# Tiles chosen in registers, x tiles that carry their own history, and result rows behind the running sum

## The chip, the core and the metric

The kernel runs on one core of a Trainium2 chip. A core has five engines with instruction streams of their own: TensorE (PE) multiplies matrices into PSUM, VectorE (DVE) and ScalarE (ACT) do elementwise work, GpSimd (POOL) does elementwise work on SBUF and issues the indirect DMAs, and SyncE (SP) issues nearly all other DMAs. Sixteen DMA engines are shared by all queues. PSUM has 8 banks of 512 float words in each of 128 partitions. The metric is the device time of one execution in microseconds (us); lower is better.

## The reference

The kernel computes a weighted sum over a window of 7 rows, and then a mixture of 8 experts in which each row goes to one.

```python
# x: (8, 3584, 192), weight_gen: (8, 3584, 8 heads, 7 taps)
w = softmax(weight_gen, axis=-1)
x_pad = concatenate([zeros(6 rows), x], axis=1)
out[b, s, h, :] = sum_k w[b, s, h, k] * x_pad[b, s + k, h, :]   # 24 columns a head

x = out.reshape(28672, 192)
logits = x @ w_gate                                   # 8 experts
e = argmax(logits); p = softmax(logits)[e]
eom = sigmoid(x @ w_output_gate)[e]
y = p * eom * (relu(x @ w1[e]) @ w2[e])               # 192 -> 1024 -> 192
```

All arrays are float32. The kernel multiplies in float16 with each operand split into a high and a low half, three products in place of one.

## The kernel before, in words

**Units.** A batch is laid out with partition p holding rows 28p to 28p + 27. A unit u is 7 of these 28 rows on every partition, so 896 rows; there are 4 units to a batch and 32 in all. For each unit DVE and ACT take the softmax of its weights (`softmax_steps`), POOL multiplies x by the weights of taps 0 to 4 (0 to 3 in units 0 to 6) and DVE by those of the others (`product`, `tap_steps`). Tap k of row j needs row j - 6 + k, which for small j lies in the tile of the unit before it or, in a batch's first unit, in a tile `halo` loaded from the partition above. So each product is made of two instructions, one on the old rows and one on the new.

**The sum.** In units 0 to 6 PE adds the seven products up through an identity matrix. From unit 7 on (`PE_U = 7`, `acc_steps`) DVE adds them in place into one running sum in PSUM words 2560 to 3903, which lie in banks 5, 6 and 7: one product is written there and six are added. `sum_steps` then reads the sum four times: ACT squares it and copies it to float16, DVE takes the low halves in two instructions. The float16 row `rt` is turned by DMA (`gt`), PE makes the logits, DVE picks the expert, and two small matmuls (`rk`) give each row its place in its expert's list. POOL scatters the rows to these places in DRAM (`srtd`), seven indirect DMAs a unit.

**Tiles.** As soon as lists hold enough rows, tiles of 512 rows of one expert are taken from them (256 and 384 early, 512 to 128 at the end; 76 tiles in all, their sizes fixed by `plan_rounds`). Which expert each tile takes is worked out at run time. `round_table` does it on DVE, on one partition, in some ten small instructions for a unit: it compares the eight counts with what was taken already, scans them and leaves the expert and the first row of each tile in a small table `ti`. SP loads these two numbers into registers (`value_load`, seen as TENSOR_LOAD) when it issues the tile's loads in `tile_load`: the rows' tokens and scales (`meta`), the rows turned (`xT`), and the expert's weights (`wa`, `wb`), each load waiting for every scatter that has been issued by then.

**The two multiplications.** `gemm_steps` sets PE's order. At each beat PE runs two units of the first multiplication (`gemm1_unit`: for a 512-row tile five matmuls of 512 columns into one bank) and one group of the second (`gemm2_group`: 24 matmuls of 192 columns for 128 result rows). ACT and DVE turn a finished bank into `hh` (relu, high half) and `hl` (low half). ACT scales a finished group into `ys`, and POOL scatters it to the output. Both multiplications take their banks from one list, `bank_free`: the banks at words 0, 512, 1024 and 1536, and four more once no unit is left. From the time that bank 1536 joins, the logits and the rank matmuls also take a bank of this list.

**What sets the order.** The kernel is written out by a planner (`Order`, `Queue`, `Paced`) while it is built. Each step is a generator with a due time; the planner keeps a clock for each engine, adds an estimated cost to it at every instruction (`vector_cost`, `scalar_cost`, `gpsimd_cost`, `sync_cost`) and always runs the step that could start first. The engines then run their streams in this fixed order, and the tile framework adds the semaphore waits between them. Every instruction that the planner records carries the line of its helper (L151 on the engines, L125 on SP).

Of the kernel before, what the change touches and what calls it, by code (L numbers as in the profile page):

```python
# [20 lines left out]
RMAX = 24  # L21
SHIFT = 15
NE = 8
# [32 lines left out]
def constants():  # L56

    ident = np.eye(P, dtype=np.float32)
    upper = np.triu(np.ones((P, P), np.float32), 1)
    r = np.arange(RMAX, dtype=np.float32)  # L60
    rr = np.tile(r[:, None], (1, 9))
    need = [T * r for T in (128, 256, 384, 512)]
    e8 = np.arange(8, dtype=np.float32) - 8.0
    flat = np.concatenate([rr.ravel(), *need, e8]).astype(np.float32)
    return np.concatenate([ident, upper, np.tile(flat[None], (P, 1))], axis=1)
# [41 lines left out]
class Queue:  # L107
# [6 lines left out]
    @property  # L114
    def t(self):
        if self.host is not None:
            return self.host.t
        return max(self.moved, self.issued + self.lead)

# [58 lines left out]
def vector_cost(name, args, kwargs):  # L178
    n = largest(args, kwargs)
    return 0.06 + n / 156.0 if name == "reciprocal" else 0.07 + n / 960.0  # L180


def scalar_cost(name, args, kwargs):
    return (0.19 if "accum_out" in kwargs else 0.1) + largest(args, kwargs) / 1200.0


def gpsimd_cost(name, args, kwargs):
    if name == "indirect_dma_start":
        return 1.2 if LOCK else 1.04
    if name == "memset":  # L190
        return 1.0
    return (0.14 if LOCK else 0.06) + largest(args, kwargs) * (0.0022 if kwargs.get("op") == ALU.add else 0.00174)
# [13 lines left out]
def sync_cost(name, args, kwargs):  # L206
# [6 lines left out]
    return n / 360e3 * (1.25 if name == "dma_start_transpose" else 1.0)  # L213
# [4 lines left out]
def kernel(ctx: ExitStack, tc: tile.TileContext, x, wg, wgate, wogate, w1, w2, cst, out):  # L218
# [47 lines left out]

    def take_place(slots):
# [20 lines left out]
    f_mx = few[:, 80:136]  # L288
    f_lim = few[0:1, 189:190]

    f_next = few[0:1, 136:152].rearrange("p (e r) -> p e r", r=2)
    f_z = few[0:1, 152:170].rearrange("p (e r) -> p e r", r=2)
    f_done = f_next[:, :, 0]
    f_ex = ps[:, 2536:2538].bitcast(I32)
    f_rr = ps[0:1, 2512 : 2512 + RMAX]

    rest_free = [(0.0, 3904), (0.0, 1344)]
    mx_free, few_free, sq_free = [0.0], [0.0], [0.0]
# [26 lines left out]
    def x_load(u):  # L325
        b, q = u // UB, u % UB
        xb = x[b].rearrange("(p j) d -> p j d", j=J)
        if q == 0:
            for lo, hi in ((1, 113), (113, 128)):
                SP.dma_start(out=halo[lo:hi], in_=xb[lo - 1 : hi - 1, J - HALO : J, :])  # L330
# [3 lines left out]
    halo = xp.tile([P, HALO, D], F32, name="halo")  # L334
    nc.gpsimd.memset(halo[0:1], 0.0)
# [7 lines left out]
    cf = cp.tile([P, cst.shape[1]], F32, name="cf")  # L343
    nc.scalar.dma_start(out=cf, in_=cst)
# [14 lines left out]
    o = 256  # L359
    rr = cf[0:1, o : o + RMAX * 9].rearrange("p (a b) -> p a b", b=9)  # L360
    o += RMAX * 9
    need = {}
    for k in (128, 256, 384, 512):
        need[k] = cf[0:1, o : o + RMAX]
        o += RMAX
    nc.vector.tensor_copy(f_e8, cf[:, o : o + 8])
# [3 lines left out]
    for e in range(NE):  # L370
        nc.vector.memset(base[:, e : e + 1], float(e * CAP - 1))
        nc.vector.memset(f_done[:, e : e + 1], float(e * CAP))


    cs = cp.tile([1, 1 + 8 * RMAX], F32, name="cs")
    nc.vector.memset(cs[:, 0:1], 0.0)
    nc.vector.memset(f_z[:, 8, :], float(DUMMY))
    nc.vector.tensor_copy(f_rr, rr[:, :, 0])
# [9 lines left out]
    state = {"base": base, "writers": [], "t": 0, "weights": 0, "rounds": 0}  # L388

# [142 lines left out]
    def product(eng, out, u, k):  # L532

        n, w4, wk = HALO - k, wloads[u], k
        if eng is V:
            w4, wk = U[u]["tw"], k - U[u]["tw_k"]
        old = halo[:, k:HALO, :] if u % UB == 0 else loads[u - 1][:, k + 1 : JS, :]
        for lo, hi, xs in ((0, n, old), (n, JS, loads[u][:, 0 : JS - n, :])):
            if hi > lo:
                eng.tensor_tensor(  # L540
                    out=out[:, lo * H : hi * H, :], in0=xs.rearrange("p j (h g) -> p (j h) g", g=GD),
                    in1=w4[:, lo * H : hi * H, wk : wk + 1].broadcast_to([P, (hi - lo) * H, GD]), op=ALU.mult)

    def softmax_steps(u):

        w4 = wloads[u]
        mxb = f_mx.unsqueeze(2).broadcast_to([P, NV, K])
        yield from take(mx_free, V)
# [21 lines left out]
        mx_free.append(od.cur.t)  # L570
# [80 lines left out]
    def used(u, tag):  # L651
# [5 lines left out]
        if "va" in d and "ga" in d:  # L657
            t = max(d["va"], d["ga"])
            x_free.extend([t] * ((u % UB > 0) + (u % UB == UB - 1)))
            w_free.append(max(d["va"], d["ga"]))  # L660
# [19 lines left out]
    def sum_steps(u):  # L680
# [84 lines left out]
        od.add(place_steps(u), (RANK_C, u, 0), V)  # L765

# [67 lines left out]

    def place_steps(u):
# [11 lines left out]
        d["rk_home"].append((od.cur.t, d["rk_at"]))  # L847
        d["ranked"] = True
        if u in plan:
            od.add(round_steps(u), (RANK_R, u), V)  # L850
        else:
            state["rounds"] += 1
# [20 lines left out]
        d["sent"] = True  # L873
        d["sent_t"] = od.cur.t + 2.5
        rt_free.append((d["sent_t"], d["ri"]))


    def round_table(r, T, R, tail, bs):

        nm = f"{r}"  # L880
        rT = need[T][:, 0:R].unsqueeze(1).broadcast_to([1, 8, R])
        if R > 2:
            n = R
            nx = sp.tile([1, 8, RMAX], F32, tag="nx", bufs=1, name=f"nx{nm}")[:, :, 0:R]
            z = sp.tile([1, 9, RMAX], F32, tag="z", bufs=1, name=f"z{nm}")[:, :, 0:R]
            V.memset(z[:, 8, :], float(DUMMY))
            V.tensor_tensor(out=nx, in0=f_done.unsqueeze(2).broadcast_to([1, 8, R]), in1=rT, op=ALU.add)
            state["step"] = None
            yield V
        else:  # L890
            if state.get("step") != T:
                state["step"] = T if R == 2 else None
                if R == 2:
                    V.tensor_scalar(f_next[:, :, 1], f_done, float(T), None, op0=ALU.add)
                    yield V
            n = 2 if state["step"] == T else 1
            nx, z = f_next[:, :, 0:n], f_z[:, :, 0:n]

        gg = sp.tile([1, 8 * RMAX], F32, tag="gg", bufs=1, name=f"gg{nm}")[:, 0 : 8 * R]
        V.scalar_tensor_tensor(out=gg.rearrange("p (e r) -> p e r", r=R), in0=bs[0:1, :].unsqueeze(2).broadcast_to([1, 8, R]), scalar=0.0 if tail else 1.0 - T, in1=nx[:, :, 0:R], op0=ALU.add, op1=ALU.is_ge)  # L900
        yield V

        if state.get("limit") != R:
            V.memset(f_lim, float(R))
            state["limit"] = R
        V.tensor_tensor_scan(out=cs[:, 1 : 1 + 8 * R], data0=gg, data1=f_lim.broadcast_to([1, 8 * R]), initial=0.0, op0=ALU.add, op1=ALU.min)
        yield V
        cx = cs[:, 0 : 1 + 8 * R : R]

        V.scalar_tensor_tensor(out=z[:, 0:8, :], in0=cx[:, 0:8].unsqueeze(2).broadcast_to([1, 8, n]), scalar=-float(T), in1=nx, op0=ALU.mult, op1=ALU.add)  # L910
        ge = sp.tile([1, RMAX, 9], F32, tag="ge", bufs=1, name=f"ge{nm}")[:, 0:R, :]
        V.tensor_tensor(out=ge, in0=cx.unsqueeze(1).broadcast_to([1, R, 9]), in1=f_rr[:, 0:R].unsqueeze(2).broadcast_to([1, R, 9]), op=ALU.is_le)
        yield V
        n = 1 if R > 2 else n
        V.scalar_tensor_tensor(out=f_next[:, :, 0:n], in0=cx[:, 1:9].unsqueeze(2).broadcast_to([1, 8, n]), scalar=float(T), in1=z[:, 0:8, 0:n], op0=ALU.mult, op1=ALU.add)
        V.tensor_tensor(out=ge, in0=ge, in1=z[:, :, 0:R].rearrange("p e r -> p r e"), op=ALU.mult)
        yield V
        if R > 8:
            ti = sp.tile([1, 2, RMAX], I32, tag="til", bufs=1, name=f"ti{nm}")
        else:  # L920
            ti = sp.tile([1, 2, 8], I32, tag="ti", bufs=NU // 2 + 6, name=f"ti{nm}")
        with nc.allow_low_precision(reason="whole numbers"):
            V.tensor_reduce(out=ti[:, 1, 0:R], in_=ge, axis=AX, op=ALU.max)
        yield V
        V.tensor_scalar(ti[:, 0, 0:R], ti[:, 1, 0:R], SHIFT, None, op0=ALU.arith_shift_right)
        yield V
        return ti
# [3 lines left out]
    def round_steps(u):  # L931

        found, bs = [], U[u]["base"]
        yield V, lambda: state["rounds"] == u
        for k, (T, R) in enumerate(plan[u]):
            tail = u == NU - 1 and k == len(plan[u]) - 1
            pads = None
            if tail:
                pads = sp.tile([1, NE], I32, tag="bi", name="bi")
                bf = sp.tile([1, NE], F32, tag="bf", name="bf")  # L940
                V.tensor_scalar(bf, bs[0:1, :], 1.0, None, op0=ALU.add)
# [322 lines left out]
XN = 4  # L1264
# [38 lines left out]
```

## Time and profile before

| what | value |
|---|---|
| three runs | 1226.5, 1228.21, 1228.29 us, median 1228.21 |
| the profiled execution | 1230.08 us, its span 1228.0 us |
| mean granted TensorE clock | 0.974 |
| busy in the span | PE 1132.9, DVE 956.4, POOL 879.8, ACT 594.5 us |
| PE idle, waiting for DVE's `hl` | 38.1 us, 40 times |
| SP waiting for scatters to `srtd` | 170.7 us, 44 times |
| first and last result read (`ys`) | 190.2 and 1220.5 us |
| last unit's sum read for the last time | 967.6 us |

The page gives busy time by engine, the chain of work that ended last, the waits and the costliest groups of instructions. A group is read as: engine, operation, what it writes and reads by the program's names, shape, count, then busy us and mean ns of one, then the idle time just before it and what ended it. `ps` is all of PSUM, so a row `ps<-ps,gap` on DVE is an addition to the running sum. Three stretches of the span follow each other: up to about 178 us the first seven units and the preparation of the weights, up to 969 us units and tiles side by side, and after it tiles alone.

### The profile page before, as it was taken

To read this page: it belongs to the slowest core of one execution; us is meant where nothing else is said; L and a number is where in the kernel's file an instruction comes from. 1 tells how busy PE (TensorE), PEld (TensorE's weight loads), DVE (VectorE), ACT (ScalarE), POOL (GpSimd) and SP (SyncE) were. 2 spreads that over 40 slices of the span, in tenths; PEclk is the share of its full clock that TensorE was granted. 3 is DMA by queue.
4 is the path that set the end of the run, shared out by engine and by line. 5 is a ranking of instruction groups with operands and counts; after the bars stand their busy time and mean duration, and the time that the engine had idled before them with its cause. 6 is when DMAs were issued, how large, how long until landed. Compare 5 with 4: busy or idle time off the path is not lost.

```text
span 1228.0 us, 27900 instructions
## 1 busy us (share of the span) xinstructions
PE 1132.9 (92%) x9710; PEld 821.3 (67%) x9710; DVE 956.4 (78%) x2027; ACT 594.5 (48%) x1263; POOL 879.8 (72%) x778
## 2 busy tenths in 40 slices
PE   5988779899999999899999999899998999999997
PEld 2444448677666666676766666676666777988987
DVE  6898759899999898998998999899998663333331
ACT  3875345455555445454544454445544544344342
POOL 5668786668888788888888988888887663322222
PEclk9998989899999999999999999999999999999999
DMA  9998378999989869698769759997777679889992
GB/s 281 284 283 288 131 237 196 262 277 250 247 232 240 206 182 248 150 262 211 213 191 229 208 154 244 231 234 188 207 203 185 178 219 278 235 255 330 272 310 80
DMA packets 278047, 279.73 MB, mean 228 GB/s; under 512 B 211479, under 2 KB 236808, under 8 KB 277905
## 3 DMA queue, kind: packets, MB, share of 16 engines
q1 hardware_dynamic: 256016, 233.35, 69.1%
q0 software_dynamic: 21744, 44.30, 13.3%
q8 instruction: 76, 1.25, 0.4%
q14 instruction: 67, 0.54, 0.1%
q10 hardware_dynamic: 144, 0.29, 0.1%
HBM read 177.07 MB, written 60.87 MB: 194 GB/s over the span
## 4 chain that ended last, share of the span: by engine, by line
PE 40%; DVE 26%; POOL 12%; issue 8%; DMA 7%; SPq 3%; ACT 3%; POOLq 0%; DVEq 0%; ACTq 0%
PE ps L151 40%; DVE ps L151 11%; POOL gap L151 6%; DVE hl L151 5%; POOL srtd L151 3%; SPq L125 3%; DMA srtd<-rt,posi 2%; POOL out_dram L151 2%; DMA wa<-wd 2%; DVE rt L151 2%; DMA gt<-rt 1%; DVE vap L151 1%; ACT rt L151 1%; DVE ti L151 1%; DVE vt L151 1%
## 5 line engine op out<-in xcount | busy, mean ns | idle before, releaser
L151 PE MATMUL ps<-xT,wa 128*128 128x512 f16 (+3 forms) x2440 | 493.0, 350 | 42.7 <-DVE hl L151 33.3
L151 PE MATMUL ps<-wb,hh 128*128 128x192 f16 x3664 | 478.9, 248 | 4.8 <-DVE hl L151 4.8
L151 PE MATMUL ps<-wb,hl 128*128 128x192 f16 x1832 | 454.1, 248 | 0.1
L151 DVE SCALAR_TENSOR_TENSOR hl<-ps,hh 128x512 f16<-128x512 f32 (+1 forms) x472 | 307.5, 665 | 156.3 <-ACT hh L151 155.9
L151 POOL TENSOR_TENSOR gap<-x,w 128x960 f32<-128x960 f32 (+5 forms) x268 | 360.0, 1368 | 37.1 <-DVE lz L151 9.2
L151 ACT ACTIVATE hh<-ps 128x512 f16<-128x512 f32 (+1 forms) x472 | 272.1, 582 | 226.1 <-PE ps L151 223.5
L151 PEld LDWEIGHTS <-wa 128*128 128x128 f16 x2440 | 226.5, 99 | 226.7 <-issue 48.8
L151 PEld LDWEIGHTS <-hh 128*128 128x128 f16 x3664 | 337.0, 99 | 50.5 <-issue 9.4
L151 POOL DMA_INDIRECT out_dram<-ys,meta x216 | 214.5, 993 | 193.6 <-ACT ys L151 146.3
L151 POOL DMA_INDIRECT srtd<-rt,posi x224 | 229.0, 1022 | 87.0 <-issue 56.4
L151 DVE TENSOR_TENSOR ps<-ps,gap 128x1344 f32<-128x1344 f32 x125 | 194.2, 1554 | 21.8 <-POOL gap L151 21.8
L151 ACT ACTIVATE ys<-ps,sc 128x192 f32<-128x192 f32 x229 | 96.3, 421 | 221.0 <-PE ps L151 160.5
L151 PEld LDWEIGHTS <-hl 128*128 128x128 f16 x1832 | 180.9, 99 | 0.6 <-DVE hl L151 0.3
L151 PE MATMUL ps<-gap,cf 128*128 128x512 f32 x168 | 72.9, 569 | 3.2 <-DVE vap L151 3.2
L151 PE MATMUL ps<-vap,cf 128*128 128x512 f32 (+1 forms) x126 | 58.2, 603 | 13.5 <-DVE vap L151 12.9
L151 POOL TENSOR_TENSOR gap<-halo,w 128x1152 f32<-128x1152 f32 (+4 forms) x38 | 60.4, 1589 | 13.2 <-issue 5.7
L151 DVE SCALAR_TENSOR_TENSOR rt<-ps,sx,rt 128x448 f16<-128x448 f32 x64 | 57.9, 908 | 10.4 <-ACT rt L151 5.8
L151 PE MATMUL ps<-xT,late 128*128 128x128 f16 (+2 forms) x600 | 56.6, 251 | 0.0
L151 ACT ACTIVATE rt<-ps 128x1344 bf16<-128x1344 f32 x32 | 41.3, 1291 | 28.2 <-issue 18.3
L151 PEld LDWEIGHTS ps<-gap,cf 128*128 128x128 f32 x168 | 31.4, 199 | 34.8 <-issue 25.6
L151 PEld LDWEIGHTS ps<-vap,cf 128*128 128x128 f32 x126 | 24.9, 208 | 38.7 <-issue 22.9
L151 ACT ACTIVATE rt<-ps,sx 128x1344 f16<-128x1344 f32 x32 | 44.2, 1380 | 9.6 <-DVE isx L151 7.6
(123 smaller groups left out, 841.8 us busy)
## 6 DMA issues: line engine op xcount, KB each, us to landing
wb<-wd SPq DMA_DIRECT2D x76, 768.5 KB
wa<-wd SPq DMA_DIRECT2D x61, 768.0 KB
x<-in_x_dram SPq DMA_DIRECT2D x32, 672.0 KB
late<-wd SPq DMA_DIRECT2D x15, 768.0 KB
wa<-wd SPq DMA_DIRECT2D x61, 128.0 KB
w<-in_wg_dram SPq DMA_DIRECT2D x32, 196.0 KB
wd<-wpb SPq DMA_DIRECT2D x8, 768.5 KB
st<-in_w_dram SPq DMA_DIRECT2D x8, 768.0 KB
```

The source lines that it names most:

```text
L125: r = f(*args, **kwargs)
L151: r = f(*args, **kwargs)
```

## The change

**Tiles in registers.** `round_table` is gone. ACT writes the eight counts of a unit as integers (`count_steps`, one more ACT instruction a unit, `cnt`), SP loads them into eight registers (`counted`), and `pick` chooses for each tile the expert with the most rows left, in register instructions of SP's own stream. A tile's loads wait for the scatters up to its own unit, not for all that were issued.

**x tiles.** A tile of x holds 13 rows a partition, the unit's 7 and the 6 before them, so a product is one instruction, and a tile is free after its own unit (`XN` 4 to 3). A load is 1248 KB where it was 672 KB; a batch's first unit loads the six rows above from a tile of zeros on partition 0.

**Result rows.** PSUM words 3904 to 4095, 192 words behind the running sum, held weights of the early units. Once these are done they become a place for one result group (`out_free`), and `take_out` gives it out ahead of the banks. The rank results keep their words in bank 4.

**The planner's costs** are changed to other numbers, and with them the order on all engines.

```diff
-        loads[u] = xp.tile([P, JS, D], F32, tag="x", bufs=XN, name=f"x{u}")
-        SP.dma_start(out=loads[u], in_=xb[:, q * JS : (q + 1) * JS, :])
+        t = loads[u] = xp.tile([P, HALO + JS, D], F32, tag="x", bufs=XN, name=f"x{u}")
...
+            SP.dma_start(out=t, in_=x[b].rearrange("(p j) d -> p j d", j=J)[:, q * JS - HALO : q * JS + JS, :])
...
-        old = halo[:, k:HALO, :] if u % UB == 0 else loads[u - 1][:, k + 1 : JS, :]
-        for lo, hi, xs in ((0, n, old), (n, JS, loads[u][:, 0 : JS - n, :])):
-            if hi > lo:
-                eng.tensor_tensor(
...
+        eng.tensor_tensor(
+            out=out, in0=loads[u][:, k : k + JS, :].rearrange("p j (h g) -> p (j h) g", g=GD),
+            in1=w4[:, :, wk : wk + 1].broadcast_to([P, NV, GD]), op=ALU.mult)
...
+    def counted(cnt):
+
+        R.reg_load(came, cnt[0:1, 0:NE])
+        for e in range(NE):
+            R.reg_alu(key[e], key[e], came[e], ALU.add)
+        SP.spend(0.6)
+
+    def pick(T):
+
+        R.reg_mov(best, (T - 1 << HAVE) + (DUMMY >> ROW))
+        for e in range(NE):
+            R.reg_alu(best, best, key[e], ALU.max)
+        for e in range(NE):
+            R.reg_alu(came[e], key[e], best, ALU.is_ge)
+            R.reg_alu(came[e], came[e], (T >> ROW) - (T << HAVE), ALU.mult)
+            R.reg_alu(key[e], key[e], came[e], ALU.add)
+        R.reg_alu(best, best, low, ALU.bitwise_and)
+        SP.spend(1.1)
+        return R.snap(best, min_val=0, max_val=DUMMY >> ROW)
...
+    def count_steps(u):
+
+        cnt = U[u]["cnt"] = sp.tile([1, NE], I32, tag="cnt", bufs=CNT, name=f"cnt{u}")
+        S.activation(cnt, U[u]["rk"][0:1, 8:16], AF.Copy, scale=float(1 << HAVE))
...
+        d["writers"] = list(state["writers"])
...
-            d = tile_load(state["t"], T, ti, i, list(state["writers"]), ka, kb)
+            d = tile_load(state["t"], T, at, U[u]["writers"], ka, kb)
...
+    def take_out():
+
+        yield T_, lambda: out_free or bank_free
+        home = out_free or bank_free
+        t, at = home.pop(0)
+        od.cur.t = max(od.cur.t, t)
+        yield T_
+        return at, home
...
-                _, at = yield from take(bank_free, T_)
+                at, home = yield from take_out()
...
+        yield T_, lambda: any(f[1] == 3904 for f in rest_free)
+        rest_free.remove(next(f for f in rest_free if f[1] == 3904))
+        out_free.append((od.cur.t, 3904))
         yield T_, lambda: "all" in state
+        yield from take(out_free, T_)
         bank_free.extend((od.cur.t, at) for at in (2560, 3072, 3584, 2048))
...
-        for _ in range(2):
-            yield from take(rk_free, T_)
...
-    return 0.06 + n / 156.0 if name == "reciprocal" else 0.07 + n / 960.0
+    return 0.15 + n / 156.0 if name == "reciprocal" else 0.15 + n / 960.0
```

Three places in the order of the two programs show what moved. In the rows a name carries its tile's number, the first number of `gap16_3` being the unit and the second the tap, that of `hl20_6` the tile and the unit of its first multiplication; in brackets are the engines and queues whose semaphores an instruction waits for.

DVE before, at the running sum of unit 16:

```order
L151 TENSOR_TENSOR ps_82<-ps_82,gap16_0_6453 128x1344 [waits DVE_49,Pool_49]
L151 SCALAR_TENSOR_TENSOR hl20_0_6595<-ps_82,hh20_0_6594 128x512 [waits Activation_49]
L151 TENSOR_TENSOR ps_82<-ps_82,gap16_1_6487 128x1344 [waits DVE_49,Pool_49]
L151 SCALAR_TENSOR_TENSOR hl20_1_6605<-ps_82,hh20_1_6604 128x512 [waits Activation_49]
L151 TENSOR_TENSOR ps_82<-ps_82,gap16_2_6591 128x1344 [waits DVE_49,Pool_49]
L151 SCALAR_TENSOR_TENSOR hl20_2_6651<-ps_82,hh20_2_6650 128x512 [waits Activation_49]
L151 TENSOR_TENSOR ps_82<-ps_82,gap16_3_6647 128x1344 [waits DVE_49,Pool_49]
L151 SCALAR_TENSOR_TENSOR hl20_3_6662<-ps_82,hh20_3_6661 128x512 [waits Activation_49]
```

DVE in the change, at the same additions:

```order
L155 TENSOR_TENSOR ps_82<-ps_82,gap16_0_6897 128x1344 [waits Activation_49,Pool_49]
L155 SCALAR_TENSOR_TENSOR hl20_6_7223<-ps_82,hh20_6_7222 128x512 [waits Activation_49]
L155 TENSOR_TENSOR ps_82<-ps_82,gap16_1_6941 128x1344 [waits DVE_49,PE_49,Pool_49]
L155 SCALAR_TENSOR_TENSOR hl20_7_7242<-ps_82,hh20_7_7241 128x512 [waits Activation_49]
L155 TENSOR_TENSOR ps_82<-ps_82,gap16_2_7001 128x1344 [waits Activation_49,Pool_49]
L155 SCALAR_TENSOR_TENSOR hl21_0_7280<-ps_82,hh21_0_7279 128x512 [waits Activation_49]
L155 SCALAR_TENSOR_TENSOR hl21_1_7293<-ps_82,hh21_1_7292 128x512 [waits Activation_49]
L155 TENSOR_TENSOR ps_82<-ps_82,gap16_3_7085 128x1344 [waits DVE_49,PE_49,Pool_49]
L155 TENSOR_TENSOR ps_82<-w17_6265,ps_82 128x112
L155 TENSOR_TENSOR ps_82<-ps_82,gap16_4_7238 128x1344 [waits Activation_49,Pool_49]
```

Before, an addition waits for DVE itself and for POOL, which makes `gap`. In the change each waits for PE or for ACT as well: the instructions waited for are the result groups of tiles 19 and 20 and their reads, which lie in the words from 3904 on, in bank 7 with the end of the sum.

ACT in the change, from the third result read of tile 19 on:

```order
L155 ACTIVATE ys19_6965<-ps_82,sc19_6966 128x192 [waits DVE_49,PE_49]
L155 ACTIVATE hh20_6_7222<-ps_82 128x512 [waits PE_49]
L155 ACTIVATE hh20_7_7241<-ps_82 128x512 [waits PE_49]
L155 ACTIVATE ys19_6965<-ps_82,sc19_6966 128x192 [waits DVE_49]
L155 ACTIVATE hh21_0_7279<-ps_82 128x512 [waits PE_49]
L155 ACTIVATE hh21_1_7292<-ps_82 128x512 [waits PE_49]
L155 ACTIVATE sc20_7304<-meta20_6405,wb20_6411 128x4 [waits DMAHW3_49]
L155 ACTIVATE ys20_7303<-ps_82,sc20_7304 128x192 [waits DMASW4_49,DMASW6_49,DMASW2_49,DMASW7_49,DVE_49,Activation_49]
```

The reads `ys` now wait for DVE too, for the addition that stands ahead of them in bank 7; before, no read waits for an addition. On PE a result group's first matmul waits likewise for the addition or the read that comes before it. Counted through the order of the change, from the first group in these words to the last read of unit 31's sum: 170 groups, 170 result reads, 173 writes of the sum (24 products and 149 additions) and 100 reads of it (50 on ACT, 50 on DVE), in one fixed sequence, which begins behind unit 7's first product and first addition. PE has 19039 rows in either program, and POOL 153 products where it had 306 pieces of them. Before, no group lies in this bank until the last unit is done; all lie in banks 0 to 3.

SP before, from the last write of prepared weights to the first tile's first load:

```order
L125 DMA wd_79<-wpb7_1081 128x1537
L125 DMA w8_1216<-in_wg_dram 128x392
L125 DMA halo_83<-in_x_dram 112x1152
L125 DMA halo_83<-in_x_dram 15x1152
L125 DMA x8_1221<-in_x_dram 128x1344
L125 TENSOR_LOAD ti2_0_1128
L125 ISA x2
L125 TENSOR_LOAD ti2_0_1128
L125 ISA x3
L125 DMA meta0_1361<-srtd_78 128x2x2
```

SP in the change, from the same write on:

```order
L129 DMA wd_79<-wpb7_1483 128x1537
L988 ISA
L129 DMA meta0_1531<-srtd_78 128x2x2
L129 ISA
L129 DMA_TRANSPOSE xT0_1533<-srtd_78 128x3x256
L129 ISA
L129 DMA wa2_136<-wd_79 128x1536
```

The first tile's loads moved ahead of unit 8's, which now stand ahead of that write; the two TENSOR_LOADs of a tile are gone.

More of the change, by code (lines that the diff above doesn't have):

```diff
@@ L20 @@
 WW = 3585
-RMAX = 24
+TURNS = 240
 SHIFT = 15
+ROW = 7
+HAVE = 11
 NE = 8
@@ L118, in t, with spend @@
         return max(self.moved, self.issued + self.lead)
+    def spend(self, us):
+        self.issued = max(self.issued, self.order.now) + us
     def __getattr__(self, name):
@@ L929 @@
     queue = []
     def round_steps(u):
[L933 to L941, printed above, removed]
-                yield V
-                V.tensor_copy(pads, bf)
-            ti = yield from round_table(f"{u}_{k}", T, R, tail, bs)
-            for i in range(R):
-                found.append((T, ti, i, pads if i == 0 else None))
```

225 lines of the change are left out of this document (90 added, 135 removed).

## The prediction

> **What bounds the kernel now.** I read the page's busy times and chain first, then three stretches, then who waits.
>
> ```profile
> PE 1132.9 (92%) x9710; PEld 821.3 (67%) x9710; DVE 956.4 (78%) x2027; ACT 594.5 (48%) x1263; POOL 879.8 (72%) x778
> PE 40%; DVE 26%; POOL 12%; issue 8%; DMA 7%; SPq 3%; ACT 3%; POOLq 0%; DVEq 0%; ACTq 0%
> ```
>
> PE leads, but the chain changes engines: no single one sets the end. The stretches (columns: length, busy us and count of PE, PEld, DVE, ACT, POOL, then granted clock, DMA share, GB/s) say where.
>
> ```profile
> 0.00:178.00 178.00, 140.97 (x584) 72.74 (x585) 133.10 (x310) 100.39 (x170) 127.57 (x106) 0.94 0.81 252
> 178.00:968.80 790.80, 740.30 (x6437) 537.20 (x6437) 731.82 (x1536) 391.02 (x878) 665.31 (x583) 0.97 0.84 217
> 968.80:1228.00 259.20, 251.66 (x2692) 211.40 (x2689) 91.48 (x185) 103.05 (x217) 86.95 (x91) 1.00 0.83 243
> ```
>
> In the last stretch PE alone is the bound. In the middle, 791 us long, PE (94%), DVE (93%) and POOL (84%) all run near their limit, and PE's idle time there is short waits for DVE:
>
> ```profile
> PE ps L151 <- DVE hl L151: 38.1, 40, 3.4
> PE ps L151 <- DMA wa<-wd: 8.1, 2, 5.9
> SPq L125 <- DMA srtd<-rt,posi: 170.7, 44, 13.8
> ```
>
> So some 46 us are all that better feeding of PE can bring; SP's long waits reach PE only as the 8.1.
>
> **What the change takes off engines that share the middle stretch.** Rows by form:
>
> ```profile
> L151 DVE TENSOR_SCALAR ti<-ti 1x2 int32<-1x2 int32 x20 | 18.6, 928 | 0.1
> L151 DVE SCALAR_TENSOR_TENSOR ps<-cs,ps 1x16 f32<-1x16 f32 x50 | 8.3, 166 | 1.4
> L151 POOL TENSOR_TENSOR gap<-x,w 128x1152 f32<-128x1152 f32 x24 | 53.8, 2242 | 26.5 <-DVE lz L151 9.2 <-DVE ez L151 8.9 <-issue 3.5
> L151 POOL TENSOR_TENSOR gap<-x,w 128x960 f32<-128x960 f32 x49 | 92.8, 1893 | 2.5 <-PE ps L151 2.2
> L151 POOL TENSOR_TENSOR gap<-x,w 128x192 f32<-128x192 f32 x32 | 17.9, 560 | 0.0
> L151 DVE TENSOR_TENSOR ps<-x,ps 128x1152 f32<-128x1152 f32 x25 | 34.1, 1362 | 0.9
> L151 DVE TENSOR_TENSOR ps<-x,ps 128x192 f32<-128x192 f32 x19 | 6.6, 347 | 0.1
> L151 DVE TENSOR_TENSOR vt<-x,ps 128x1344 f32<-128x1344 f32 x25 | 38.6, 1543 | 0.1
> ```
>
> Choosing tiles leaves DVE: 27 us in the two rows shown, and I estimate 50 with the smaller ones. A product in one piece: on DVE 1.54 for 1.36 + 0.35, 0.17 x 39 = 6 us; on POOL 192 columns more cost 2242 - 1893 = 349 ns, so one piece of 1344 takes 2.59 where two took 2.24 + 0.56 = 2.80, 0.21 x 153 = 32 us. This would relieve the middle stretch if these engines stayed its bound.
>
> The cost of the loads: 32 loads of 1248 KB for 32 of 672 and 8 halos of 571.5 are 14 MB more.
>
> ```profile
> x<-in_x_dram SPq DMA_DIRECT2D x32, 672.0 KB
> halo<-in_x_dram SPq DMA_DIRECT2D x8, 504.0 KB
> ```
>
> That is 5% of all bytes at a DMA share of 0.84; five of the first seven units take 0.59 MB more each, 12 us of DMA at 252 GB/s, beside a stretch that PE and DVE also fill. I take 0, with 0 to 12 as bounds. SP's register instructions and its one load of counts a unit have no row; they replace two loads a tile, and what queues behind SP are prefetches for which PE waited 8.1 us in all: 0, bounds -8 to +8. ACT gains 32 small instructions at 48% busy: 0.
>
> **The result rows are what decides.** PE's steady beat, in the timeline of the last stretch (start, length):
>
> ```profile
> 1010.31 0.33 PE L151 MATMUL ps<-wb,hh 128*128 128x192 f16 x2
> 1012.29 2.32 PE L151 MATMUL ps<-xT,wa 128*128 128x512 f16 x10
> 1012.49 0.42 ACT L151 ACTIVATE ys<-ps,sc 128x192 f32<-128x192 f32 x1 [1.38 <-PE ps L151]
> 1014.45 0.33 PE L151 MATMUL ps<-wb,hh 128*128 128x192 f16 x2
> ```
>
> A beat is 4.14 us: a result group of 2.0 and ten matmuls of the first multiplication. A group holds its bank from 1010.31 until its read ends at 1012.91. In the change this bank is bank 7, where the sum ends, and the order shows that additions wait for groups and reads, and these for additions, though their words differ. That such a wait is real is seen before in bank 4, where logits (words 2048 on) and the softmax's words (2400 on) meet:
>
> ```profile
> 155.33 0.57 DVE L151 TENSOR_REDUCE ps<-w 128x56 f32<-128x392 f32 x1 [0.59 <-ACT w L151]
> 155.95 0.30 PE L151 MATMUL ps<-gm,gt 128*128 128x32 f16 x6 [1.23 <-DVE ps L151]
> 156.28 0.23 DVE L151 TENSOR_SCALAR ps<-ps 128x56 f32<-128x56 f32 x1 [0.39 <-PE ps L151]
> 203.37 1.56 DVE L151 TENSOR_TENSOR ps<-ps,vt 128x1344 f32<-128x1344 f32 x1
> 205.02 1.29 ACT L151 ACTIVATE rt<-ps 128x1344 bf16<-128x1344 f32 x1 [0.49 <-DVE ps L151]
> ```
>
> PE's logits start 0.05 after DVE's last word of the bank, DVE goes on 0.03 after PE, and ACT starts 0.09 after DVE in the last two rows: a hand-over is 0.03 to 0.09, I take 0.05. The Trainium skill ("PSUM — Partial Sum Buffer", section "PSUM bank collisions raise a hardware error") says that two engines must not touch one bank together even at different columns, and that semaphores should guard banks, not addresses. The trace agrees in these rows; guarding by address would leave the first rival's time below.
>
> The holders of bank 7, by form:
>
> ```profile
> L151 DVE TENSOR_TENSOR ps<-ps,gap 128x1344 f32<-128x1344 f32 x125 | 194.2, 1554 | 21.8 <-POOL gap L151 21.8
> L151 ACT ACTIVATE rt<-ps,sx 128x1344 f16<-128x1344 f32 x32 | 44.2, 1380 | 9.6 <-DVE isx L151 7.6 <-DVE sx L151 1.7
> L151 ACT ACTIVATE rt<-ps 128x1344 bf16<-128x1344 f32 x32 | 41.3, 1291 | 28.2 <-issue 18.3 <-DVE ps L151 8.2 <-DVE ti L151 0.8
> L151 DVE SCALAR_TENSOR_TENSOR rt<-ps,sx,rt 128x896 f16<-128x896 f32 x32 | 36.3, 1136 | 0.0
> L151 DVE SCALAR_TENSOR_TENSOR rt<-ps,sx,rt 128x448 f16<-128x448 f32 x32 | 21.8, 680 | 10.4 <-ACT rt L151 5.8 <-DMA wa<-wd 2.5 <-DMA srtd<-rt,posi 0.5
> ```
>
> The sequence counted in the order of the change has 170 groups, 170 result reads, 173 writes of the sum, 50 reads of it by ACT (1.34 each) and 50 by DVE (0.91). Between two groups PE needs 4.14; the bank needs 2.0 + 0.42 and whatever stands between. In 81 of the 170 intervals that fits: with one write, 2.0 + 0.42 + 1.55 + 3 hand-overs = 4.12. In 37 there are two writes: 2.0 + 1.55 + 0.42 + 1.55 + 4 hand-overs = 5.72, 1.58 over, 58 us. In the other 52 stand reads of the finished sum or more writes, 0.25 to 6.1 over, 82 us. So the stretch takes 170 x 4.14 + 140 = 844 us at least; 827 with free hand-overs, 863 with 0.09.
>
> Before, the same work ran in 776 us:
>
> ```profile
> L151 ACT ACTIVATE ys<-ps,sc x166: 401/421/451, 190.2 to 966.7; 128x192 f32<-128x192 f32 x166
> 189.86 1.55 DVE L151 TENSOR_TENSOR ps<-ps,gap 128x1344 f32<-128x1344 f32 x1
> 178.00:968.80 790.80, 19.09 (x525) 0.00 (x0) 0.00 (x0) 0.97 0.84 217
> ```
>
> To the 844 I add what such a chain doesn't hold. PE's logits, 19 us in this stretch (third row), hide in the intervals that are over: half, 10. DVE is in order, and one or two `hl` (0.68 each) stand between two writes where I counted a read of 0.42: 0.26 or 0.94 in 43 intervals, 11 to 40, I take 20. Of the waits and the lower clock before, 776 - 166 x 4.14 - 19 = 70, most lie now under the longer intervals: 15, bounds 0 to 70. That makes 45, bounds 10 to 130.
>
> **Start and end.** The first group stands behind unit 7's first addition, which ran before at 189.86. Tile loads that start earlier don't help, since PE waits there; fewer DVE and POOL us in the first units pull it forward, larger loads push it back: 190, bounds 175 to 200. After unit 31's sum 63 reads took 259 us before; now 59 are left: 259 - 4 x 4.14 = 242.
>
> **Sum.** 190 + 844 + 45 + 242 = 1321 of span; 2 us lie outside it, and the median of the runs stood 2 below the profiled execution: 1321 us. By the bounds: 175 + 827 + 10 + 240 = 1252, and 200 + 863 + 130 + 245 = 1438.
>
> **Rivals.**
> *The sharing is hidden and the relief counts.* If groups and additions met by chance rarely, PE would lose its waits for `hl` and `wa`: 1228 - 46 = 1182, with half of it 1205. For it: four banks are left to the first multiplication, and DVE and POOL lose some 55 and 32 us of work. Against it: the waits stand in the program, in a sequence that 89 times does not fit. It decides only if the 140 us were under 40.
> *The chain feeds on itself.* An addition that waits for a group holds up every `hl` behind it on DVE, and the next group waits for these; and PE's clock falls when it idles:
>
> ```profile
> 300.00:320.00 20.00, 18.29 (x165) 14.28 (x164) 19.25 (x51) 10.37 (x29) 18.26 (x16) 1.00 1.01 278
> 780.00:800.00 20.00, 15.91 (x128) 10.34 (x127) 15.46 (x18) 5.53 (x13) 16.59 (x16) 0.89 0.93 201
> ```
>
> At 0.9 the groups alone cost 170 x 0.2 = 34 us more, and `hl` at its upper bound 20: with some other waits 1390.
> *A lighter chain.* The sum stands, but units start at 175 and the additions hide: 1262.
> *Nothing to measure.* Relief and sharing cancel: 1228. That needs both of the first two at half strength, which nothing suggests.
>
> **How the numbers follow.** Forecast (1285 to 1350) 0.62, self-feeding chain 0.17, lighter chain 0.12, hidden sharing 0.06, nothing 0.03. A measurement here tells 0.2% from no change, so faster 0.06, same 0.03, slower 0.91. The range 1255 to 1385 takes in the lighter chain and half of the heavier.
>
> **What would show it.** Right: PE's waits for DVE (additions) and ACT (`ys`) in the middle stretch grow from 38 to over 100 us, DVE's additions show idle time released by PE and ACT, first and last `ys` around unit 31's sum lie 860 to 920 us apart, and the clock falls there. Wrong: additions start without such waits, or the middle stretch stays under 790 us. A first result read well before 180 would put my start wrong.

## The result

The changed kernel takes 1689.4 us (median of 4 runs, 1689.1 to 1692.9) where the kernel before takes 1228.3 on the same chip: 1.377 times as long, interval 1.374 to 1.379. The forecast was 1321, with 1255 to 1385 as the range. The sign was right; the size was not: 461 us more instead of 93.

The profiled execution of the changed kernel took 1689.1 us, its span is 1687.3. From its page, busy times and the chain:

```profile
PE 1167.2 (69%) x9710; PEld 827.2 (49%) x9710; DVE 920.9 (55%) x1683; ACT 584.9 (35%) x1295; POOL 858.8 (51%) x624
PE 25%; DVE 7%; SPq 6%; issue 4%; DMA 2%; ACT 2%; POOL 0%; DVEq 0%; POOLq 0%; ACTq 0%
```

Every engine does about as much as before, DVE and POOL a little less; none is busy for more than 69%. So the loss is waiting, and PE's waits (us in total, times, longest) say for what:

```profile
PE ps L155 <- DVE ps L155: 108.5, 67, 4.1
PE ps L155 <- DMA wa<-wd: 108.1, 8, 39.6
PE ps L155 <- DMA gt<-rt: 96.8, 5, 35.2
PE ps L155 <- DVE rt L155: 65.6, 18, 47.0
PE ps L155 <- DVE vap L155: 62.3, 4, 58.4
```

The first row is the wait that the prediction was about: many short ones. The others are few, the longest of each 35 to 58 us, for transfers or for engines that themselves waited for transfers. The prediction had nothing of that length. The waits of that length lie at eight places. Windows of 60 us at three of them, and the sum over such windows at all eight (columns as before: length, busy us and count of PE, PEld, DVE, ACT, POOL, then granted clock, DMA share, GB/s):

```profile
0.00:60.00 60.00, 1.58 (x2) 0.84 (x3) 7.53 (x20) 2.41 (x5) 5.79 (x16) 1.00 0.23 77
...
225.00:285.00 60.00, 26.53 (x138) 14.13 (x136) 27.34 (x66) 18.01 (x37) 35.58 (x23) 0.73 0.25 87
440.00:500.00 60.00, 15.09 (x131) 11.37 (x129) 11.46 (x29) 9.36 (x23) 16.66 (x11) 0.67 0.58 86
...
sum 480.00, PE 161.14 PEld 98.36 DVE 148.88 ACT 85.39 POOL 154.51; mean PE 20.14 PEld 12.29 DVE 18.61 ACT 10.67 POOL 19.31
```

Everything stands nearly still there, on all engines at once, and the memory traffic of these three falls to 77 to 87 GB/s. The view of the transfers in the third, in 40 slices of 1.5 us, shows at which rate (`DMA` is the busy share of the 16 DMA engines in tenths, 0 being less than one):

```profile
DMA  9421102202202002000000029000000000299999
GB/s 408 148 91 67 46 23 95 89 31 86 89 35 93 27 24 29 27 27 27 27 27 27 27 49 90 27 27 27 27 27 27 27 27 27 60 205 319 285 302 332
```

The full slice at the start moves 408 GB/s. From 459.5 to 491 the rate is 24 to 29 in all but two slices, about a fifteenth of it; in the 15 us ahead of that it is 95 at most. And SP's timeline shows what was issued ahead of it and what stuck:

```profile
436.07 0.78 SPq L129 DMA_DIRECT2D x<-in_x_dram  x2
...
444.37 18.33 SPq L129 DMA_DIRECT2D meta<-srtd  x1
462.86 29.13 SPq L129 DMA_TRANSPOSE xT<-srtd  x1
...
987.45 47.47 SPq L129 DMA_TRANSPOSE gt<-rt  x7
```

At 436 SP issues the x tile of a batch's first unit. The next issues, which take 0.4 and 1.5 us elsewhere, take 18 and 29, and in another such place seven transposes take 47. Seven such transposes in the kernel before:

```profile
182.02 9.98 SPq L125 DMA_TRANSPOSE gt<-rt  x7
```

The page's list of transfers names the load: eight of them, one for each batch.

```profile
x<-in_x_dram SPq DMA_DIRECT2D x8, 1238.2 KB
```

In a batch's first unit the change loads partition 0 apart and partitions 1 to 127 in one load: 127 partitions of 9984 bytes. 1238.2 KB (1.268 MB) at 27 GB/s are 47 us, as long as SP stands at the two slow issues (444.4 to 492.0). The kernel before loaded its halo for the same partitions as 112 and 15. Because of these loads the first result read is late too:

```profile
L155 ACT ACTIVATE ys<-ps,sc x229: 396/421/424, 309.4 to 1680.1; 128x192 f32<-128x192 f32 x115
```

309.4 where it was 190.2, because three of the eight loads fall into the first 230 us.

### The profile page after: what moved, and what is told of

It is laid out like the page before. It is cut to its first block, busy times and chain, and to the rows that moved or that the text cites. A ratio compares the mean times of both kernels' runs of the same rounds, so it can differ in the third digit from the quotient of the medians.

```text
span 1687.3 us, 27560 instructions
## 1 busy us (share of the span) xinstructions
PE 1167.2 (69%) x9710; PEld 827.2 (49%) x9710; DVE 920.9 (55%) x1683; ACT 584.9 (35%) x1295; POOL 858.8 (51%) x624
## 5 line engine op out<-in xcount | busy, mean ns | idle before, releaser
L155 PE MATMUL ps<-xT,wa 128*128 128x512 f16 (+3 forms) x2520 | 520.7, 357 | 113.3 <-DMA wa<-wd 108.1
L155 POOL TENSOR_TENSOR gap<-x,w 128x1344 f32<-128x1344 f32 x153 | 397.6, 2604 | 101.5 <-DMA x<-in_x_dram 53.4
L155 PEld LDWEIGHTS <-wa 128*128 128x128 f16 x2520 | 237.1, 100 | 308.2 <-DMA wa<-wd 109.7
L155 ACT ACTIVATE hh<-ps 128x512 f16<-128x512 f32 (+1 forms) x472 | 267.8, 582 | 292.3 <-PE ps L155 290.7
L155 DVE TENSOR_TENSOR ps<-ps,gap 128x1344 f32<-128x1344 f32 x125 | 195.6, 1565 | 107.3 <-ACT ys L155 38.1
L155 PE MATMUL ps<-gm,gt 128*128 128x32 f16 x672 | 28.4, 179 | 116.4 <-DMA gt<-rt 96.8
L155 PEld LDWEIGHTS <-gt 128*128 128x128 f16 x672 | 25.1, 98 | 127.5 <-DMA gt<-rt 101.0
L155 DVE TENSOR_TENSOR vap<-x,ps 128x1344 f32<-128x1344 f32 x21 | 32.4, 1545 | 87.5 <-DMA x<-in_x_dram 49.3
L155 DVE TENSOR_REDUCE lz<-ps 128x112 f32<-128x224 f32 x32 | 12.3, 385 | 109.7 <-PE ps L155 109.7
L155 DVE TENSOR_REDUCE ps<-w 128x56 f32<-128x392 f32 x64 | 36.3, 566 | 57.6 <-DMA w<-in_wg_dram 53.1
## 6 DMA issues: line engine op xcount, KB each, us to landing
x<-in_x_dram SPq DMA_DIRECT2D x8, 1238.2 KB
```

The lines of the kernel that those rows point to most:

```text
L155: r = f(*args, **kwargs)
```

## The experiments

Eighteen runs on five chips. Ratios are against the kernel before, run beside them on the same chip. On four of the chips the kernel before takes 1227 to 1230 us. On the fifth it takes 1298, so times from that chip are read only as ratios, and what was to be compared with other chips was run again.

### The two suspects: the load of 127 partitions, and the shared bank

**Loads of 112 and 15.** The changed kernel with

```diff
-            SP.dma_start(out=t[1:P], in_=x[b, J - HALO : P * J - HALO, :].rearrange("(p j) d -> p j d", j=J)[:, 0 : HALO + JS, :])
+            src = x[b, J - HALO : P * J - HALO, :].rearrange("(p j) d -> p j d", j=J)[:, 0 : HALO + JS, :]
+            for lo, hi in ((1, 113), (113, 128)):
+                SP.dma_start(out=t[lo:hi], in_=src[lo - 1 : hi - 1])
```

> The changed kernel, but the load of partitions 1 to 127 that opens each group of four units (1238.2 KB, eight times) goes as two loads of 112 and 15 partitions. Theory A (that load runs on one of the 16 DMA engines: the trace of the changed kernel shows 27 GB/s in stretches of about 46 us, and 1238.2 KB / 27 GB/s = 46 us, x 8 = 367 us): 1689 - 367 = 1322 us, 1290 to 1370, and no stretch at 27 GB/s. Rival B (the loss is the bank shared by the sum and the result rows, larger than I summed it): the time stays above 1600 us.

**Groups in free banks.** The changed kernel with

```diff
-        yield T_, lambda: out_free or bank_free
-        home = out_free or bank_free
+        yield T_, lambda: bank_free
+        home = bank_free
```

> The changed kernel, but every result group takes a free bank as before the change; the loads of 127 partitions stay. Theory A: the stretches at 27 GB/s stay, the bank's part of the loss goes, and that part is at most the 93 us that I forecast, some of it lying under the stalls: 1690 less 40 to 115, 1575 to 1650 us. Rival B: 1300 us or less.

**Both edits.**

> Both edits: loads of 112 and 15 partitions, and result groups in free banks. What is left of the change is the tiles chosen in registers, the tiles of 13 rows, and the order by measured durations. By my prediction's rival without sharing: 1182 to 1205 us, up to 1228 if the relief is worth nothing. If neither cause holds, it stays above 1300 us.

Measured, from 1689.4: loads alone 1402.9 us (ratio 1.142, 1.140 to 1.145), banks alone 1580.9 (1.287, 1.283 to 1.290), both 1266.8 (1.030, 1.026 to 1.034). So the load costs 286 us with the shared bank in place and 314 without it, the bank 108 and 136; both together 423 of the 461. Rival B falls. Theory A holds in kind, but 1403 lies above its 1290 to 1370: what it left over was larger than I had summed. The kernel with both edits, at 1266.8, is also above the 1182 to 1228 expected.

With the loads split, the same windows of time read:

```profile
0.00:60.00 60.00, 41.41 (x120) 20.25 (x121) 40.54 (x66) 25.26 (x40) 34.27 (x26) 1.00 0.83 253
...
225.00:285.00 60.00, 44.46 (x400) 34.34 (x398) 45.32 (x76) 20.37 (x57) 21.52 (x14) 0.94 0.91 228
440.00:500.00 60.00, 45.93 (x398) 32.01 (x397) 45.45 (x88) 26.15 (x60) 44.92 (x33) 0.97 0.96 244
...
sum 480.00, PE 369.12 PEld 243.04 DVE 331.71 ACT 198.40 POOL 293.07; mean PE 46.14 PEld 30.38 DVE 41.46 ACT 24.80 POOL 36.63
```

PE is busy for 369 us of these 480, where it was for 161. No stretch stands still, and nothing but the cut of eight loads was changed by hand (the planner's order moved with it). The Trainium skill ("DMA: Bandwidth & Descriptors", section "Why a DMA increments its semaphore by 16 and not by 1") says that a transfer runs on the largest number of DMA engines, 16 at most, that divides the outer dimension of both its sides: 127 partitions on one, and by the same rule 112 on 16 and 15 on 15. The trace agrees: 27 GB/s for the one, with less than a tenth of the 16 engines' time busy, and 408 in a full slice. Which engine it was no view shows, and of the sizes only 127 against 112 and 15 was run.

That kernel is also the one in which the shared bank can be seen by itself. PE's waits in it, and then in the kernel with both edits:

```profile
PE ps L155 <- DVE ps L155: 110.7, 70, 4.1
...
PE ps L155 <- DVE rt L155: 25.7, 18, 7.5
PE ps L155 <- ACT rt L155: 18.0, 13, 2.5
```

```profile
PE ps L155 <- DMA wa<-wd: 59.1, 10, 14.1
...
PE ps L155 <- DVE ps L155: 11.9, 9, 3.7
PE ps L155 <- DVE hl L155: 11.1, 10, 5.1
```

PE's waits for additions to the sum (`ps`) and for reads of it (`rt`) are 154 us with groups in bank 7 and 14 without (11.9 for `ps`, and 2.4 for `rt` further down). One piece of its timeline, split loads, groups in bank 7 (start, length, idle before and what ended it):

```profile
560.20 1.57 DVE L155 TENSOR_TENSOR ps<-ps,gap 128x1344 f32<-128x1344 f32 x1 [0.42 <-ACT ys L155]
...
561.82 0.33 PE L155 MATMUL ps<-wb,hh 128*128 128x192 f16 x2 [1.73 <-DVE ps L155]
...
564.00 0.42 ACT L155 ACTIVATE ys<-ps,sc 128x192 f32<-128x192 f32 x1 [2.56 <-PE ps L155]
...
565.95 0.33 PE L155 MATMUL ps<-wb,hh 128*128 128x192 f16 x2
...
568.13 1.57 DVE L155 TENSOR_TENSOR ps<-ps,vt 128x1344 f32<-128x1344 f32 x1 [0.66 <-PE ps L155]
...
569.74 0.42 ACT L155 ACTIVATE ys<-ps,sc 128x192 f32<-128x192 f32 x1 [2.98 <-DVE ps L155]
...
570.29 1.29 ACT L155 ACTIVATE rt<-ps 128x1344 bf16<-128x1344 f32 x1
...
571.73 0.33 PE L155 MATMUL ps<-wb,hh 128*128 128x192 f16 x2 [0.94 <-ACT rt L155]
```

Addition, group, read of its result, a second group, addition, read of the second result, read of the finished sum, third group: one holder after the other. Where the rows show the end of a holder and the start of the next, 0.04 to 0.15 us lie between them. The result read of 569.74 had its group finished before 568.13, and stood behind an addition to other words of the bank.

### The same two edits, each alone in the kernel before

**One load of 127 partitions**, where the halo was loaded in two:

```diff
-            for lo, hi in ((1, 113), (113, 128)):
+            for lo, hi in ((1, 128),):
```

> The kernel before, but each halo goes as one load of 127 partitions (571.5 KB, eight times) where it was two of 112 and 15. Theory A: 571.5 KB / 27 GB/s = 21 us on one engine, x 8 = 169 us, of which the later ones are partly hidden: 1228 + 80 to 170 = 1308 to 1398 us. Rival (the tiles of 13 rows, their longer packets or their 14 MB, are what slows the changed kernel): 1228 us within 5.

1355.9 us, ratio 1.104 (1.100 to 1.108): inside the expected 1308 to 1398, and far from the rival's "within 5". No x tile was changed, so the larger tiles are not needed for the loss; one outer size is enough.

**Result rows behind the sum.** `take_out`, `out_free` and the `home` of a group as in the change, nothing else:

```diff
-                _, at = yield from take(bank_free, T_)
+                at, home = yield from take_out()
```

> The kernel before with one thing added: result groups take the 192 words behind the running sum, as in the change. By the first call the shared bank costs 1403 - 1267 = 136 us with the rest of the change; if that is the bank alone it costs about as much here, 1228 + 100 to 150 = 1328 to 1378 us (my prediction's sum said 93). If it needs the rest of the change, 1228 to 1260 us.

On the slower chip 1459.9 against 1298.3: ratio 1.126 (1.120 to 1.131), 162 us there, above the 100 to 150 expected. So the bank doesn't need the rest of the change for its cost; whether it costs the same 136 by itself this run can't say, since it was run on the slower chip only.

### What is left: 3%

With both mended the kernel still lost 39 us. Four parts of the change were left: x tiles of 13 rows, the planner's durations, tiles chosen in registers, shorter lists of waits.

**7-row tiles.** Both mended, with `x_load`, `product`, the halo and `XN = 4` of before.

> Both causes mended (loads of 112 and 15 partitions, groups in free banks: 1267 us) and besides the x tiles of before: 7 rows, four buffers, a halo, products in two pieces. Theory L (the 39 us that remain come from the larger tiles: 14 MB more, and three buffers where there were four, so that the loads of weights for the tiles come late): 1215 to 1235 us. Otherwise 1260 us or more.

**Old durations**, with the 13-row tiles; and then **both**, old tiles and old durations (the durations of the other engines and of SP go back in the same way):

```diff
-    return 0.15 + n / 156.0 if name == "reciprocal" else 0.15 + n / 960.0
+    return 0.06 + n / 156.0 if name == "reciprocal" else 0.07 + n / 960.0
...
```

> Both causes mended (1267 us) and besides the planner's durations of before. Theory C (the new durations give an order in which the tiles' weights are asked for late): 1215 to 1240 us. Under theory L: 1255 to 1275 us.

> Both causes mended, and both the x tiles and the planner's durations of before: what is left of the change is the tiles chosen in registers, with loads that wait for fewer writes. Theory R (choosing in registers takes some 50 us of small instructions off DVE, and is a gain): 1195 to 1225 us. Rival S (SP waits in its queue for each unit's counts, and tiles come late whatever the loads): 1240 us or more.

On the slower chip the ratios were 0.992 (0.988 to 0.995), 1.034 (1.030 to 1.039) and 1.002 (0.9998 to 1.005). That looked like theory L, and like a kernel that beats both. It was neither: on a chip like the others the same kernels read otherwise. Two of the runs again, on such a chip, and two more:

> The same kernel as the one with both causes mended and the x tiles of before, run again as a base on the chip of this call. It was 0.9915 of the kernel before on the last chip; 0.985 to 0.998 here.

> The same kernel as the one with both causes mended and the tiles of 13 rows, so that the x tiles are compared on one chip. It was 1.030 of the kernel before on another chip. If the larger tiles cost what the two calls say, it is 3 to 4.5% above the one with tiles of 7 rows; if that difference was the chips', under 1.5%.

**Late counts.** 7-row tiles, and SP reads a unit's counts later:

```diff
-        yield SP, lambda: state["rounds"] == u and "counted" in U[u]
+        yield SP, lambda: state["rounds"] == u and "counted" in U[u] and "sent" in U[u]
```

> The kernel with tiles of 7 rows, but SP reads a unit's counts when the unit's rows have been sent instead of as soon as they are counted. Before this edit SP waited 112 us in all for counts in the middle stretch, with prefetches of weights queued behind, and PE waited 69 us for these. If SP's waits are what makes the weights late (rival S): PE's wait falls under 30 us and the time by 15 to 40 us, ratio 0.96 to 0.98. If not: within 0.7% of the kernel it is made from.

**The bytes alone.** 7-row tiles and, with every other instruction in the same order:

```diff
+        if q:
+            nc.sync.dma_start(out=waste, in_=xb[:, q * JS - HALO : q * JS, :])
```

> The kernel with tiles of 7 rows and, in the same order of everything else, a load of 6 further rows (576 KB) into a tile that nobody reads, for the 24 units that have no halo: the 14 MB of the larger tiles alone. If the bytes are what the larger tiles cost: 2.5 to 4.5% above the kernel it is made from. If it is something else (the order that the planner then chooses, the longer runs): under 1.5%.

7-row tiles 1262.5 us, ratio 1.027 (1.023 to 1.030); 13-row tiles 1266.2, 1.031 (1.028 to 1.035); the bytes alone 1265.7, 1.031 (1.028 to 1.034). So with the new durations the larger tiles or their 14 MB cost 3 to 4 us, hardly more than the runs of one kernel differ, and theory L falls: my bounds of 0 to 12 us were right for the bytes. Late counts made it slower, which neither expectation had, 1285.4 and 1.046 (1.041 to 1.051): PE's wait for weights stayed (71.8 us), so that wait isn't cured by moving the counts, and rival S in that form falls too.

> Both causes mended, tiles of 13 rows, the planner's durations of before; run before only on the chip where the kernel before takes 1298 us (1.0343 there). If the new durations are what makes the rest of the loss: 0.99 to 1.01. If they don't matter: 1.025 to 1.04, as with the new ones (1.031).

> Both causes mended, tiles of 7 rows, the planner's durations of before, so that registers that choose the tiles and the waits for fewer writes are what is left (1.0022 on the slower chip). If the new durations make the rest of the loss: 0.98 to 1.005. If choosing in registers does (SP waiting for counts): 1.02 to 1.04.

**New durations alone**, in the kernel before (the diff above the other way round, and the other engines' durations):

> The kernel before, with the new durations for the planner and nothing else. If these make the rest of the loss: 1.02 to 1.04 (1253 to 1278 us). If not: 0.99 to 1.01.

**Waits for all rows**, on the kernel with old tiles and old durations:

```diff
-            d = tile_load(state["t"], T, at, U[u]["writers"], ka, kb)
+            d = tile_load(state["t"], T, at, list(state["writers"]), ka, kb)
```

> As the one with tiles of 7 rows and the durations of before, but a tile's loads wait for all rows sent so far, as before the change. If the shorter list of waits is worth something: 0.5 to 2% above the kernel it is made from. If the tiles are asked for late anyway, behind SP's other waits: within 0.5% of it.

Ratios: 1.038 (1.034 to 1.041), 1.028 (1.026 to 1.031), 1.041 (1.038 to 1.045), 1.029 (1.026 to 1.031). With the old durations the 13-row tiles cost 11 us (1274.5 against 1263.7), more than the 3 to 4 above and still inside the bounds. The shorter lists of waits are worth nothing (1263.0 with the long ones, 1263.7 with the short). The new durations alone cost 49 us in the kernel before (1278.4 against 1229.6). But the registers with the old durations cost 34 as well, and both together no more. That could mean that any order but the tried one costs 3%, so two other orders were drawn.

```diff
-    return 0.06 + n / 156.0 if name == "reciprocal" else 0.07 + n / 960.0
+    return 0.06 + n / 156.0 if name == "reciprocal" else 0.08 + n / 960.0
```

> The kernel before, with one number of the planner changed by 10 ns: a VectorE instruction's fixed duration 0.08 where it was 0.07. Nothing of the work changes, but 1350 lines of VectorE's order and 134 of SP's read otherwise. If the 3 to 4% that remains of the loss is the price of leaving an order that was found by trying (every other order of this planner costs about as much): 1.015 to 1.04. If it comes from the new durations or the registers as such: within 1% of before.

> The same in the other direction, 0.06 where it was 0.07: a second draw. Theory of the tried order: again 1.015 to 1.04. Otherwise within 1%.

1225.9 us with 0.08 (ratio 0.9987, 0.997 to 1.0004) and 1233.8 with 0.06 (1.005, 1.002 to 1.007). The theory of the tried order falls in the form that every other order costs as much: two that differ in over a thousand lines of DVE's are within 0.5%. So the new durations and the register part each bring a cost of their own, and each leaves its mark in PE's waits. New durations in the kernel before:

```profile
PE ps L151 <- DMA wa<-wd: 70.8, 14, 13.6
PE ps L151 <- DVE vap L151: 13.2, 2, 11.8
PE ps L151 <- DVE hl L151: 11.7, 12, 3.4
```

Before, PE waited 38.1 us for `hl` and 8.1 for weights. With the new durations the wait for `hl` falls to 11.7 and the weights come late, 70.8; the four kernels with both mended and new durations that ran on chips like the first show 58 to 72. What makes SP ask late in that order was not tried.

Registers with old durations and old tiles instead show PE waiting at the rank matmul. The same group, in the kernel before and in this one (count, busy, mean ns, idle before):

```profile
L151 PE MATMUL ps<-p,upper 128*128 128x8 f16 x32 | 5.7, 177 | 4.5 <-DVE ps L151 4.1 <-DVE p L151 0.2
```

```profile
L155 PE MATMUL ps<-p,upper 128*128 128x8 f16 x32 | 5.6, 174 | 36.9 <-DVE ps L155 18.7 <-DVE w L155 12.3 <-DVE p L155 3.6
```

32 us more at this group. Its timeline at one of them:

```profile
515.83 0.27 DVE L155 TENSOR_TENSOR_SCAN p<-segs,ps 128x56 f16<-128x56 f16 x1
...
520.93 0.57 DVE L155 TENSOR_REDUCE ps<-w 128x56 f32<-128x392 f32 x1 [4.01 <-DMA w<-in_wg_dram]
...
521.55 0.17 PE L155 MATMUL ps<-p,upper 128*128 128x8 f16 x1 [4.17 <-DVE ps L155]
```

The matmul's input `p` is there at 516.10. It starts at 521.55, 0.05 after a reduction of the next softmax, which had waited 4.01 for its weights to land. Both write words of bank 4: the change keeps the ranks there, where the kernel before gave them a free bank. It is the shared bank a second time, read from the trace; giving the ranks a free bank was not run. What it costs isn't measured by this: the row puts another 12.3 and 3.6 us down to `w` and `p`, in the same kernel PE's wait for `hl` is 7.8 shorter and its wait for weights 13.0 longer than before, and the kernel with the long lists loses as much with 27.5 us at this group.

A second mark of the registers is the choosing itself. A `pick` takes SP 1.23 us, and behind the last unit's counts 23 of them stand in a row. In the kernel with both mended SP reads these counts at 1041.3 and issues the next tile's first load at 1080.35; between them lie the 23 picks, 28 us, and the eight writes that fill the lists up. PE stands for it:

```profile
1088.10 4.45 PE L155 MATMUL ps<-xT,wa 128*128 128x512 f16 x10 [14.10 <-DMA wa<-wd]
```

With old tiles and old durations this wait is 11.3 us; the kernel before and the one with the new durations alone have none at this point. That too is read from the traces: no run chose the last tiles in another way.

No run of these beats the kernel before on a chip like the first by more than can be measured.

## Why the prediction was wrong

By its steps:

- **The loads: wrong, and the step that failed.** "I take 0, with 0 to 12 as bounds" priced the bytes and only these: right for them (3 us), but the shape of eight loads cost 286. The row to stop at was quoted there: the halo went in eight loads of 504.0 KB, which are 112 partitions, with the other 15 loaded apart. The prediction took the 1248 KB of one load as moving like any other and didn't ask why the old code cut at 113. With that load cut in two, the rest of the change takes 1403, still above the range: the terms below are 8, 59 and 12 us short (start, stretch, tail).
- **The start at 190: wrong for the same reason**, 309 with the uncut loads; 197.6 with them cut, inside its 175 to 200.
- **The shared bank: right in kind, and nearly in size.** The sum said 889 us from the first result read to the end of unit 31's sum, 113 more than before. Split loads have 948 there (197.6 to 1145.9), both mended 816 (201.1 to 1016.9), the kernel before 779: the bank is worth 132 there and 136 in the whole. What was missing is mostly the other 37, which both mended show too: 7 more groups in the stretch (29), and the waits below.
- **The tail: 242 forecast, 254 measured** with split loads, and 249 with both mended, though 57 and 56 reads are left there and not 59. The 4.14 a beat that carried it doesn't hold across the hand-over from units to tiles: with both mended PE idles there for the 14.1 us shown above, behind SP's picks.
- **The planner's durations: a term that the sum didn't have.** It treated the new numbers as if only the places of the instructions that it named would move. Alone they cost 49 us.
- **SP's registers and counts: "0, bounds -8 to +8": too narrow.** With old durations and old tiles the part costs 34 us. The traces put some of it to the ranks that share bank 4 and 11 to SP's picks; the split between them is not shown. The 76 picks take SP 1.23 us each, and the sum took them as free since they replace two loads a tile.
- **DVE's relief: overstated.** 956 to 921 busy, 35 less, where I had 56. It bought nothing that a run shows: with both mended PE's wait for `hl` fell to 11.1 while others took its place.
- **The signs to look for** held where the loads are cut: waits for additions and reads 154 us ("over 100"), and DVE's additions idle for PE (66.5 us) and for ACT (43.2). The granted clock is lower, 0.962 against 0.974, but speaks for nothing here: both mended, without the shared bank, have 0.954. The first and the last result read around unit 31's sum are 947 apart, outside the 860 to 920.

Of the rivals, none was the result. The kernel without the uncut loads landed at 1403, past the range and near the 1390 of the "chain that feeds on itself". That is chance: that rival went by a clock of 0.9, and 0.962 was granted.

## What to carry to other kernels

Before a transfer's bytes are priced, look at its outer dimension: 127 partitions in one load moved at 27 GB/s, and the loads issued behind it stood for 47 us, and all engines with them. Where old code cuts something oddly, find out what the cut was for before pricing its removal. In this kernel's waits a tile's bank, not its words, is the unit in PSUM: before results are put beside something else in a bank, write the holders in order and add them up against the beat, and do so for every tenant that the change moves, the small ones too. And a choice that moves into SP's own stream takes SP's time: put a price on each and count how many stand in a row ahead of a load.

## What was not expected of the hardware

One slow load holds up the issue of later ones as well as their data: SP needed 47.47 us to issue seven transposes where seven take it 9.98 in the kernel before.

One chip of those used is 5.7% slower for the kernel before (1298 us) and 1.8% for the one with both mended and 7-row tiles (1285 against 1262), so that their ranking turns round. In that kernel, DVE's wait ahead of `hl` that no event explains was, on the slower chip and then on the other:

```profile
DVE hl L155 <- issue: 39.5, 36, 2.4
```

```profile
DVE hl L155 <- issue: 0.4, 1, 0.4
```

What delays an engine there for 1 us at a time stays open. A ratio of a few per cent between two kernels held on one chip and not on the other.
